# Clustered attention with an MLP: another order of the opening, with norms behind one-hot evictions and the first pair's scores between row maxima

## The chip, the cores and the metric

The kernel runs on one core of one Trainium2 chip. A core has a matmul engine (TensorE, PE in the profile; its weight loads are listed as PEld), VectorE (DVE), ScalarE (ACT), GpSimd (POOL) and SyncE (SP), which issues most of the DMAs; ACT issues a few. All of them work out of SBUF, PE writes to PSUM, and each engine takes its own instructions in program order. The metric is the device time of one execution in microseconds (us), lower is better; a kernel's time is the median over several executions.

## The reference

Attention in which a query sees only the keys of its own cluster, then a low-rank mix over the sequence, then a channel MLP with a residual. Batch 4, 8 heads, 768 positions, head size 64, 16 clusters, model size 512, hidden size 2048, all fp32:

```python
q_assign = np.argmax(np.einsum('bhsd,hcd->bhsc', q_n, c_n), axis=-1)   # q_n, k_n, c_n: rows of length 1
k_assign = np.argmax(np.einsum('bhsd,hcd->bhsc', k_n, c_n), axis=-1)
mask = q_assign[:, :, :, None] == k_assign[:, :, None, :]
scores = np.where(mask, scale * np.matmul(q, k.transpose(0, 1, 3, 2)), -1e9)
attn = softmax(scores)                     # row maximum taken off, exp, divided by the sum
x = np.matmul(attn, v)                     # then heads side by side: (B, S, 512)
u = x + (x^T @ U @ V)^T
out = u + np.maximum(u @ w_ch1, 0.0) @ w_ch2
```

## The kernel before

Two heads of one batch form a pair; there are 16 pairs, numbered from 0. Of every pair the program makes the same chain of steps, each a small function of the source:

- `load` brings queries and keys (tile `R`), `split_hi` (L375, ACT) and `split_lo` (L380, POOL or DVE) cut them into a high and a low part in a large tile `arena`, and `place_keys_hi`, `place_keys_lo`, `place_queries` (DMAs, L217) put the parts on the partitions where the matmuls want them.
- `sims` (L330 on PE, L333 on ACT) gives the similarity to the centroids; ACT's eviction multiplies by the centroids' inverse norms `c_rn`, which `norms` (L279 to L287, eight small DVE operations with one square root on ACT, L281) makes, once for pair 0's centroids and once for those of the three other pairs of heads. `turn_centroids` (L268, L271) transposes the centroids.
- `largest` and `clusters` (PE transposes L340, then five DVE operations L344, L345, L352, L353, L356) find the cluster of every query and key and write it as a one-hot tile `oh`.
- The one-hots go to partitions 64 to 96 of `arena`. For pair 0 alone this is `turn_clusters` (PE L422, evictions on ACT L429 and DVE L426). For the others it is `clusters_T` (six PE transposes L365, ACT eviction L367 to `ohT`) and `place_clusters` (four DMAs of `ohT` on SP's queue).
- `rowmax` (PE L440, DVE L442) makes, for 12 blocks of queries times two halves of the keys, the block of masked scores and its row maximum. `rowmax_T` and `rowmax_place` (L447, PE L452, ACT L454, a DMA of `mT` on ACT's queue) turn 6 or 12 columns of maxima into a row of `arena`, which the second matmuls of `scores` then subtract.
- `scores` (PE L464 and L466, exp on ACT L469 into `pr`), `weights` (sums of `pr` into `T`, L479, POOL and at a few places DVE) and `values` (PE L487, eviction L491) run 12 times per pair: two halves `h` of the queries, six key blocks `c` each. `sums`, `sums_T` and `normalise` finish the pair.

After the last pair of a batch come the mix, and after all pairs the MLP, which fills the second half of the time.

Nothing plans the order at run time. Each step is put in a list with a time (a plain number), the list is sorted by it, and the functions are called in that order; `keep_order` then ties each engine to the order of the calls. The times come from tables (one row per step, one column for pair 0, 1, 2, the last of a batch, the last of all and the rest). The first steps of all, on pairs 0 and 1, are written out by hand in the list `start`. Pair 0's scores have times from -0.47 up in steps of 1, its values come in groups of six, the transposes of pair 1's one-hots (`clusters_T`) have -0.09.

PSUM has four banks under the names `ps_...` and `o_ps`, and two tiles of two banks under `st`; a matmul into a bank waits until the bank's last reader is done.

Of the kernel before, what the change touches and what calls it, by code (L numbers as in the profile page):

```python
# [53 lines left out]
GV = 6  # L54
# [63 lines left out]
def clustered_attention_moe(ctx: ExitStack, tc: tile.TileContext, qk, v, cen, moe_U, moe_V, w1, w2, out):  # L118
# [820 lines left out]
    def at(time, fn, *args):  # L939
        plan.append((time, len(plan), fn, args))  # L940
# [3 lines left out]
        (table, AF.Sqrt), (load_centroids, 0, 1), (turn_centroids, 0), (load, 0, 0), (load, 0, 1),  # L944
        (load_centroids, 1, 4), (load, 1, 0), (load, 1, 1), (norms, 0, 1), (split_hi, 0, 0),
        (split_hi, 0, 1), (place_keys_hi, 0), (sims, 0), (split_lo, 0, 0), (split_lo, 0, 1),
        (constants, 0), (place_ones, 0), (largest, 0), (place_keys_lo, 0), (clusters, 0), (norms, 1, 4),
        (turn_centroids, 1), (turn_clusters, 0, 1), (place_queries, 0), (turn_centroids, 2),
        (turn_centroids, 3), (turn_clusters, 0, 0), (constants, 1), (sims, 1), (rowmax, 0, 0),
        (table, AF.Exp), (rowmax, 0, 2), (split_hi, 1, 0), (split_hi, 1, 1), (rowmax, 0, 5),  # L950
        (rowmax, 0, 1), (rowmax, 0, 4), (load_v, 0), (rowmax, 0, 3), (rowmax_T, 0, 0, 6),
        (rowmax_place, 0, 0, 6), (largest, 1), (split_lo, 1, 0), (split_lo, 1, 1), (clusters, 1),
# [7 lines left out]
    def kind(i):  # L960
        name = ("first", "second", "third")[i] if i < 3 else (
            "last" if i == n - 1 else "last of a batch" if i % NP == NP - 1 else "most")
        return kinds.index(name)

    def when(name, i):
        return NS * i + times[name][kind(i)]

    for i in range(n):
        if i > 1:
            for h in range(2):  # L970
                for fn in (load, split_hi, split_lo):
                    at(when(f"{fn.__name__}{h}", i), fn, i, h)
            for fn in (sims, largest, clusters, place_keys_hi, place_keys_lo, place_queries, place_ones):
                at(when(fn.__name__, i), fn, i)
        if i:
            for fn in (clusters_T, place_clusters, load_v):
                at(when(fn.__name__, i), fn, i)

        pace = (0.5, 0.75, 0.75, 1)[min(i, 3)]
        for u in range(NT if i == 0 else 0, NS):  # L980
            for h in range(2):
                if i < 3:
                    at(when("rowmax", i) + pace * u + 0.01 * h, rowmax, i, u, h)
                else:
                    g, r = divmod(2 * u + h, 2 * GV)
                    at(when("rowmax", i) + GV * g + spots[r], rowmax, i, u, h)
        if i == 1:
            at(when("rowmax_T", i) - 4, rowmax_T, i, 0, NT)
            at(when("rowmax_place", i) - 5, rowmax_place, i, 0, NT)
        u0 = NT if i < 2 else 0  # L990
        at(when("rowmax_T", i), rowmax_T, i, u0, NS)
        at(when("rowmax_place", i), rowmax_place, i, u0, NS)
        for k in range(NS):
            h, c = divmod(k, NT)
            at(when("scores", i) + k, scores, i, h, c)
            at(when("values", i) + GV * (k // GV) + GV - 1 + 0.001 * (k % GV), values, i, h, c)
            if c:
                at(when("weights", i) + k, weights, i, h, c)
        at(when("sums", i), sums, i)
        at(when("sums_T", i), sums_T, i)  # L1000
        for h in range(2):
            at(when(f"normalise{h}", i), normalise, i, h)
# [31 lines left out]
    for n_, (g, k) in enumerate((g, k) for g in range(NG) for k in range(2)):  # L1034
        c = M0 + (3 + 3.1 * n_ if n_ < 7 else 26.3)
# [17 lines left out]
    for b in range(1, B):  # L1053
# [17 lines left out]
        for k, (which, x) in enumerate(seq):  # L1071
# [20 lines left out]
            elif x < 6 or b < B - 1:  # L1092
                first = sorted(order[1].index(key) for key in order[b < B - 1][0:3])
# [44 lines left out]
```

## Time and profile before

| | |
|---|---|
| median of 3 runs | 1011.31 us (1010.62 to 1015.38) |
| profiled execution | 1008.9 us, of which 1007.1 us are the span of the profile |
| busy in the span: PE, DVE, ACT, POOL | 95%, 71%, 47%, 60% |
| attention (pairs 0 to 15) | from 0 to about 440 us |
| the opening that the change touches | from about 8 to 46 us |

The prediction shows lines of four views: the page; busy time by stretches (`us, PE busy (x) PEld busy (x) DVE busy (x) ACT busy (x) POOL busy (x), PEclk, DMA share, GB/s`, where PEclk is the granted clock of PE, 1 being full); the timeline (start in us, duration in us, engine, line, operation, tiles, sizes, count, and in brackets how long the engine sat idle before and what released it); and the order of the instructions. A row of the timeline with `x12` covers twelve instructions in a row and its duration is that of all twelve. A `q` behind an engine's name marks the queue that issues DMAs; the duration is that of the issuing.

### The profile page before, as it was taken

The page shows a single profiled execution, that of the slowest core. Times are in us where ns is not written, and L with a number is a line of the kernel's source. Part 1 is how long each engine was busy: PE and PEld are TensorE (multiplying, and loading weights), DVE is VectorE, ACT ScalarE, POOL GpSimd, SP SyncE. Part 2 cuts the span into 40 slices and gives each one's busy share as a digit, 9 for nine tenths or more (in the row PEclk, how much of TensorE's full clock was granted, in tenths as well). Part 3 has the DMA queues.
Part 4 walks back from the last instruction along what each step waited for, and adds up shares of the span by engine and source line. Part 5 has one row for each costly group of instructions (what it writes and reads, how often), then busy time and mean ns, then how long its engine had stood idle before and what let it go on. Part 6 is the DMA issues. An engine that isn't in the chain of part 4 may idle for free. (4 is left out here: it accounts for less than half of the span.)

```text
span 1007.1 us, 15377 instructions
## 1 busy us (share of the span) xinstructions
PE 953.1 (95%) x5368; PEld 778.0 (77%) x5368; DVE 715.1 (71%) x1322; ACT 472.0 (47%) x837; POOL 601.5 (60%) x453
## 2 busy tenths in 40 slices
PE   5899999999999999988988998999999899999997
PEld 3565665676666756656777887899999899999997
DVE  5797777777787667666788524765688666886767
ACT  4454555565555645464456534453344433443330
POOL 5466676889678868753356846742375623855330
PEclk9899999999999999989999999999999999999999
DMA  7754653655676644347477995877677776677744
GB/s 183 193 130 119 162 148 93 201 156 151 152 213 170 153 116 144 96 134 235 142 232 232 322 349 187 329 266 271 231 261 260 274 295 239 229 280 267 248 147 146
DMA packets 76733, 205.29 MB, mean 204 GB/s; under 512 B 8624, under 2 KB 42416, under 8 KB 71792
## 3 DMA queue, kind: packets, MB, share of 16 engines
q1 hardware_dynamic: 73968, 195.82, 60.9%
q10 hardware_dynamic: 2688, 8.49, 2.8%
q8 instruction: 42, 0.69, 0.3%
q14 instruction: 35, 0.29, 0.1%
HBM read 131.07 MB, written 41.94 MB: 172 GB/s over the span
## 5 line engine op out<-in xcount | busy, mean ns | idle before, releaser
L442 DVE TENSOR_REDUCE m<-ps_max 128x1 f32<-128x384 f32 x384 | 195.5, 549 | 82.6 <-PE ps_max L440 81.2
L479 POOL TENSOR_TENSOR T<-T,pr 128x768 f32<-128x768 f32 x120 | 225.7, 1881 | 46.1 <-ACT pr L469 19.5
L469 ACT ACTIVATE pr<-st 128x768 f32<-128x768 f32 x192 | 154.6, 813 | 85.7 <-PE st L466 69.0
L487 PE MATMUL o_ps<-pr,vt 128*64 128x384 f32 x768 | 132.9, 496 | 0.1
L440 PE MATMUL ps_max<-arena 128*128 128x384 f32 x384 | 126.6, 380 | 6.7 <-DVE oh L356 2.5
L464 PE MATMUL st<-arena 128*128 128x384 f32 x384 | 105.0, 354 | 1.9 <-ACT pr L469 1.8
L440 PEld LDWEIGHTS ps_max<-arena 128*128 128x128 f32 x384 | 70.5, 192 | 45.4 <-issue 21.4
L487 PEld LDWEIGHTS o_ps<-pr,vt 128*64 128x64 f32 x768 | 52.9, 138 | 66.9 <-issue 60.3
L466 PE MATMUL st<-arena 97*128 97x384 f32 x384 | 99.7, 341 | 4.6 <-DMA arena<-mT 2.6
L479 POOL TENSOR_TENSOR T<-pr 128x768 f32<-128x768 f32 x30 | 56.6, 1885 | 64.9 <-ACT pr L469 64.9
L464 PEld LDWEIGHTS st<-arena 128*128 128x128 f32 x384 | 66.3, 190 | 17.8 <-issue 9.9
L466 PEld LDWEIGHTS st<-arena 97*128 97x128 f32 x384 | 70.4, 190 | 6.2 <-issue 4.5
L491 ACT COPY os<-o_ps 128x384 f32<-128x384 f32 x32 | 15.4, 480 | 105.4 <-PE o_ps L487 105.4
L800 PE MATMUL ps_p<-arena,w 128*128 128x384 f32 x186 | 62.3, 335 | 0.1
L801 PE MATMUL ps_p<-arena,w 128*128 128x384 f32 x186 | 62.2, 334 | 0.0
L802 PE MATMUL ps_p<-arena,w 128*128 128x384 f32 x186 | 62.2, 334 | 0.0
L800 PE MATMUL ps_q<-arena,w 128*128 128x384 f32 x150 | 50.1, 334 | 0.0
L802 PE MATMUL ps_q<-arena,w 128*128 128x384 f32 x150 | 50.1, 334 | 0.0
L801 PE MATMUL ps_q<-arena,w 128*128 128x384 f32 x150 | 50.1, 334 | 0.0
L380 POOL TENSOR_TENSOR arena<-R,arena 128x768 fp32r<-128x768 f32 x18 | 34.4, 1918 | 13.5 <-ACT arena L375 7.9
L665 POOL TENSOR_TENSOR f<-f 128x512 f32<-128x512 f32 x8 | 10.3, 1293 | 52.1 <-DVE f L660 52.1
L607 DVE SCALAR_TENSOR_TENSOR hx<-ps_h,hx 128x384 fp32r<-128x384 f32 x32 | 17.7, 554 | 29.0 <-ACT hx L606 28.9
(541 smaller groups left out, 2444.3 us busy)
## 6 DMA issues: line engine op xcount, KB each, us to landing
w<-wc SPq DMA_DIRECT2D x24, 1024.0 KB
w<-wc SPq DMA_DIRECT2D x24, 768.0 KB
wc<-f SPq DMA_DIRECT2D x52, 256.0 KB
arena<-wc SPq DMA_DIRECT2D x17, 768.0 KB
R<-in_qk SPq DMA_DIRECT2D x32, 384.0 KB
arena<-arena SPq DMA_DIRECT2D x32, 384.0 KB
arena<-arena SPq DMA_DIRECT2D x64, 192.0 KB
arena<-wc SPq DMA_DIRECT2D x10, 1024.0 KB
```

The source lines that it names most:

```text
L380: eng.tensor_sub(part(X2[i % 3], 0, h), live["R", i][:, 2 * h:2 * h + 2].rearrange("p j q -> p (j q)"), part(X1[i % 3], 0, h))
L440: nc.tensor.matmul(ps[:, 0:HS], x1[:, 0, g // 2, g % 2, t * P:(t + 1) * P], x1[:, 1, h, g % 2, :], start=True, stop=True)
L442: nc.vector.reduce_max(live["m2", i][:, h, u:u + 1], ps[:, 0:HS], axis=AX.X)
L464: nc.tensor.matmul(st[:, j, 0:HS], x1[:, 1, hk, j, ks], x1[:, 0, h, j, :], start=True, stop=False)
L466: nc.tensor.matmul(st[:, j, 0:HS], x2[0:97, 1, hk, j, ks], x2[0:97, 0, h, j, :], start=False, stop=True)
L469: nc.scalar.activation(pr, st[:, :, 0:HS], AF.Exp, scale=SCALE)
L479: eng.tensor_add(T, live["p", i, h, 0] if c == 1 else T, live["p", i, h, c])
L487: nc.tensor.matmul(o_ps[64 * j:64 * j + 64, 0:HS], vv[:, c, j, :], pr[:, j, :], start=(c == 0), stop=(c == NT - 1))
L607: nc.vector.scalar_tensor_tensor(out=hl, in0=ps[:, 0:HS], scalar=0.0, in1=hh, op0=ALU.max, op1=ALU.subtract)
L800: nc.tensor.matmul(ps, w[:, 0, k], u[:, 0, k], start=(k == 0), stop=False)
L801: nc.tensor.matmul(ps, w[:, 0, k], u[:, 1, k], start=False, stop=False)
L802: nc.tensor.matmul(ps, w[:, 1, k], u[:, 0, k], start=False, stop=(k == 1))
```

## The change

Two edits, both in the order alone; every instruction is the same as before.

In the list `start`, the norms of the later centroids (`norms, 1, 4`) and their transposes move behind pair 0's one-hots (`turn_clusters`), and `sims` of pair 1 behind the first row maximum:

```diff
-        (constants, 0), (place_ones, 0), (largest, 0), (place_keys_lo, 0), (clusters, 0), (norms, 1, 4),
-        (turn_centroids, 1), (turn_clusters, 0, 1), (place_queries, 0), (turn_centroids, 2),
-        (turn_centroids, 3), (turn_clusters, 0, 0), (constants, 1), (sims, 1), (rowmax, 0, 0),
+        (constants, 0), (place_ones, 0), (largest, 0), (place_keys_lo, 0), (clusters, 0),
+        (turn_clusters, 0, 1), (place_queries, 0), (turn_clusters, 0, 0), (constants, 1), (turn_centroids, 1),
+        (rowmax, 0, 0), (turn_centroids, 2), (turn_centroids, 3), (norms, 1, 4), (sims, 1),
         (table, AF.Exp), (rowmax, 0, 2), (split_hi, 1, 0), (split_hi, 1, 1), (rowmax, 0, 5),
```

Pair 0's first six scores, exps and sums get times between those of the row maxima of its second half, and all its first values the time -2, which is ahead of `clusters_T` of pair 1:

```diff
         for k in range(NS):
             h, c = divmod(k, NT)
-            at(when("scores", i) + k, scores, i, h, c)
-            at(when("values", i) + GV * (k // GV) + GV - 1 + 0.001 * (k % GV), values, i, h, c)
+            first = i == 0 and h == 0
+            at(-8.99 + 0.5 * k if first else when("scores", i) + k, scores, i, h, c)
+            at(-2 if first else when("values", i) + GV * (k // GV) + GV - 1 + 0.001 * (k % GV), values, i, h, c)
             if c:
-                at(when("weights", i) + k, weights, i, h, c)
+                at(-8.7 + 0.5 * k if first else when("weights", i) + k, weights, i, h, c)
```

What this does to the engines, read from the built programs. On DVE, in the opening (`m_276` and `m_252` are the same tile of row maxima, `oh_127` is pair 0's one-hots), a minus stands before what is gone from a place and a plus before what is new there:

```order
 L356 TENSOR_TENSOR oh_127<-ps_simT,rank 128x24x16
+L426 TENSOR_SCALAR arena<-st,osc,obi 32x2x384 x2
+L442 TENSOR_REDUCE m_252<-ps_max 128x1 x2
 L279 TENSOR_TENSOR rw_g<-rw_g 128x192
 L280 TENSOR_REDUCE c_n_135<-rw_g 128x3
...
 L287 RECIPROCAL c_rn<-c_n_134 128x3
-L426 TENSOR_SCALAR arena<-st,osc,obi 32x2x384 x2
-L442 TENSOR_REDUCE m_276<-ps_max 128x1 x12
-L447 TENSOR_REDUCE m<-m_276 128x6
+L442 TENSOR_REDUCE m_252<-ps_max 128x1 x10
+L447 TENSOR_REDUCE m<-m_252 128x6
```

The eight operations of the norms, which stood ahead of the two evictions L426, now stand behind these and behind the first two of the twelve row maxima. The rest of DVE's order is as it was.

On PE, from the transposes for pair 1's clusters on, before (`oh_128` is pair 1's one-hots):

```order
L340 MATMUL ps_simT<-ident,sims 128x128 x3
L440 MATMUL ps_max<-arena 128x384 x12
L464 MATMUL st<-arena 128x384 x2
L466 MATMUL st<-arena 128x384 x2
L365 LDWEIGHTS oh_128
L365 MATMUL ps_oh<-ident_b,oh_128 128x128
```

and with the change, from the last of six scores on:

```order
L464 MATMUL st<-arena 128x384 x2
L466 MATMUL st<-arena 128x384 x2
L487 MATMUL o_ps<-pr,vt 64x384 x12
L365 LDWEIGHTS oh_128
L365 MATMUL ps_oh<-ident_b,oh_128 128x128
...
L452 MATMUL ps_mT<-ident,m 6x128
L330 MATMUL ps_sim<-R,cT 32x384 x4
L340 MATMUL ps_simT<-ident,sims 128x128 x3
L440 MATMUL ps_max<-arena 128x384 x6
L464 MATMUL st<-arena 128x384 x2
```

Before, pair 1's transposes L365 came behind one score of pair 0, and the five others, the values and a seventh score stood behind them, among L452, L330 and L340 of pair 2 and the row maxima L440 of pair 1. Now all six scores (spread among the last eight row maxima of pair 0) and the values stand ahead of L365; behind it there is no score until six row maxima of pair 1 are through. From the next row on PE's two orders are the same.

On ACT with the change, from the first exp on:

```order
L469 ACTIVATE pr<-st 128x768 x6
L491 COPY os<-o_ps 128x384
L367 ACTIVATE ohT<-ps_oh,obi,osc 128x768
L454 ACTIVATE mT<-ps_mT 6x128
L217 DMA arena<-mT 1x6x128
L333 ACTIVATE sims<-ps_sim,c_rn 128x384
L375 CAST arena<-R 128x768 x3
```

Before, the eviction L367 of pair 1's one-hots came behind the first exp, and L333 of pair 2 and the three casts L375 of later pairs stood between the others. SP issues the same DMAs in the same order as before.

## The prediction, made before the changed kernel was run

> **What bounds the kernel now.** I read the page first, then busy time by stretches, then the timeline of the opening engine by engine, since only the opening is edited.
>
> ```profile
> PE 953.1 (95%) x5368; PEld 778.0 (77%) x5368; DVE 715.1 (71%) x1322; ACT 472.0 (47%) x837; POOL 601.5 (60%) x453
> L469 ACT ACTIVATE pr<-st 128x768 f32<-128x768 f32 x192 | 154.6, 813 | 85.7 <-PE st L466 69.0
> ```
>
> ```profile
> 17.00:33.00 16.00, 11.61 (x32) 7.06 (x31) 14.68 (x31) 3.59 (x6) 3.59 (x2) 0.71 0.78 208
> 33.00:46.00 13.00, 12.23 (x73) 7.87 (x72) 7.63 (x14) 8.95 (x13) 9.73 (x5) 0.97 0.55 127
> 46.00:60.00 14.00, 13.60 (x80) 8.53 (x77) 11.58 (x21) 6.59 (x11) 7.02 (x5) 1.00 0.49 131
> 60.00:75.00 15.00, 14.06 (x75) 10.03 (x75) 14.15 (x34) 8.61 (x14) 11.01 (x7) 1.00 0.62 160
> 100.00:150.00 50.00, 49.19 (x299) 33.78 (x300) 37.76 (x76) 27.74 (x41) 34.99 (x20) 1.00 0.59 151
> ```
>
> PE is the bound of the whole. In the opening it is not: from 17 to 33 us DVE is (14.68 of 16), and from 33 to 46 us neither DVE nor ACT is full. From 46 us on PE or DVE is always nearly full. So a delay that exists at 46 us has hardly any hole to disappear in, and the question is when the first row that is common to both orders again can run: PE's L440 behind pair 0's first values, at 46.28. DVE's timeline up to there:
>
> ```profile
> 11.80 0.35 DVE L279 TENSOR_TENSOR rw_g<-rw_g 128x192 f32<-128x192 f32 x1
> 13.92 0.17 DVE L287 RECIPROCAL c_rn<-c_n 128x3 f32<-128x3 f32 x1
> 14.52 1.07 DVE L426 TENSOR_SCALAR arena<-st,osc,obi 32x768 fp32r<-32x768 bf16 x1 [0.42 <-ACT arena L429]
> 16.52 1.07 DVE L426 TENSOR_SCALAR arena<-st,osc,obi 32x768 fp32r<-32x768 bf16 x1 [0.93 <-ACT arena L429]
> 17.62 5.67 DVE L442 TENSOR_REDUCE m<-ps_max 128x1 f32<-128x384 f32 x12
> 23.33 0.17 DVE L447 TENSOR_REDUCE m<-m 128x6 f32<-128x12 f32 x1
> 27.01 0.56 DVE L356 TENSOR_TENSOR oh<-ps_simT,rank 128x384 bf16<-128x384 f32 x1
> 38.58 0.56 DVE L344 TENSOR_REDUCE mx<-ps_simT 128x24 f32<-128x384 f32 x1 [5.24 <-PE ps_simT L340]
> 39.65 2.87 DVE L442 TENSOR_REDUCE m<-ps_max 128x1 f32<-128x384 f32 x6
> 42.43 2.02 DVE L380 TENSOR_TENSOR arena<-R,arena 128x768 fp32r<-128x768 f32 x1
> 45.57 0.56 DVE L356 TENSOR_TENSOR oh<-ps_simT,rank 128x384 bf16<-128x384 f32 x1
> ```
>
> The norms (11.80 to 14.09) lie in a hole: the eviction behind them waits for ACT anyway, 0.42 us. The large hole is the 5.24 us before L344 of pair 2. PE:
>
> ```profile
> 18.24 3.70 PE L440 MATMUL ps_max<-arena 128*128 128x384 f32 x8 [0.36 <-DVE m L442]
> 27.71 4.31 PE L440 MATMUL ps_max<-arena 128*128 128x384 f32 x9 [2.25 <-DVE oh L356]
> 31.82 0.84 PE L464 MATMUL st<-arena 128*128 128x384 f32 x2
> 33.11 0.86 PE L365 MATMUL ps_oh<-ident_b,oh 128*128 128x128 bf16 x6
> 35.51 0.85 PE L330 MATMUL ps_sim<-R,cT 128*32 128x384 f32 x8
> 39.43 0.52 PE L464 MATMUL st<-arena 128*128 128x384 f32 x2
> 39.79 0.51 PE L466 MATMUL st<-arena 97*128 97x384 f32 x2
> 40.14 1.49 PE L440 MATMUL ps_max<-arena 128*128 128x384 f32 x4
> 42.26 4.09 PE L487 MATMUL o_ps<-pr,vt 128*64 128x384 f32 x24
> 46.28 0.30 PEld L440 LDWEIGHTS ps_max<-arena 128*128 128x128 f32 x2 [0.60 <-DVE oh L356]
> ```
>
> PE sits behind L356 twice: at 27.71 (pair 1's one-hots) and at 46.28 (pair 2's, done at 45.57 + 0.56 = 46.13). The chain that leads to the second starts with L365 at 33.11, and its other links are on ACT and in a queue:
>
> ```profile
> 16.80 0.58 ACT L333 ACTIVATE sims<-ps_sim,c_rn 128x384 f32<-128x384 f32 x1 [0.31 <-PE ps_sim L330]
> 18.80 1.55 ACT L375 CAST arena<-R 128x768 fp32r<-128x768 f32 x2
> 34.07 0.99 ACT L367 ACTIVATE ohT<-ps_oh,obi,osc 128x768 fp32r<-128x768 bf16 x1
> 35.09 2.62 SPq L217 DMA_DIRECT2D arena<-ohT  x4
> 35.65 0.25 ACT L454 ACTIVATE mT<-ps_mT 6x128 fp32r<-6x128 f32 x1
> 35.93 0.68 ACTq L217 DMA_DIRECT2D arena<-mT  x1
> 37.37 0.57 ACT L333 ACTIVATE sims<-ps_sim,c_rn 128x384 f32<-128x384 f32 x1
> 38.90 0.36 PEld L440 LDWEIGHTS ps_max<-arena 128*128 128x128 f32 x2
> ```
>
> Today PE does its scores while that chain runs.
>
> **Step 1, the norms.** Eight operations, 2.29 us from 11.80 to 14.09, free today, now between row maxima two and three, where DVE is the bound: +2.3. In return the second L429 no longer waits behind casts of L271, so L426 can end about half a microsecond sooner; the first L440 waits for copies by DMA too, which do not move. I give back 0.5 (between 0 and 0.6): **+1.8** (1.7 to 2.3). The first half of the maxima ends at 23.50 + 1.8 and L356 of pair 1 at 27.57 + 1.8 = 29.4; only PE transposes and five DVE operations lie between. Late behind the norms is also ACT's L333 of pair 1 (it needs `c_rn`: about 20.4 for 16.80), and with it the casts L375, POOL's L380 and SP's copies, by some 3.6 us. Their next reader on PE is pair 1's first row maximum, which comes later still (step 3). I cost that at nothing; without that cover it would be 3.6.
>
> **Step 2, PE from the gate to the end of the values.** The gate at 27.71 goes to 29.5. From there PE now does one L440, six scores, eight L440 in twos and 24 L487. At full clock two L464 take 0.36 (39.43 to 39.79), so do two L466 and two L440; a score is 0.71 (39.43 to 40.14); the values take 46.13 - 42.26 = 3.87. Sum: 0.18 + 6 x 0.71 + 4 x 0.36 + 3.87 = 9.75. DVE (0.47 per maximum, 5.67 / 12) keeps up, and so does ACT (813 ns an exp, in the second row of the page above). The values would end at 39.3. But the clock:
>
> ```profile
> 20.00:22.00 2.00, 1.84 (x5) 0.74 (x4) 2.00 (x6) 0.35 (x1) 2.00 (x2) 1.00 0.23 52
> 24.00:26.00 2.00, 1.47 (x6) 0.96 (x4) 1.39 (x3) 0.17 (x1) 0.00 (x0) 0.50 1.01 212
> 33.00:34.00 1.00, 1.00 (x8) 0.90 (x8) 0.31 (x2) 0.66 (x1) 0.00 (x0) 0.56 0.57 216
> 34.00:35.00 1.00, 1.00 (x7) 0.91 (x7) 0.00 (x0) 1.00 (x3) 0.00 (x0) 1.00 0.03 12
> ```
>
> PE runs at half clock from before 24 to about 33.9 us: it drops while the matmuls are paced by DVE, and is full again some 2 us after dense work began (31.82). A score at half clock takes 31.82 to 33.11, 1.29. The paced stretch stays, with gaps like today's, so I take half clock again, from 29.5 to about 33.9: 4.4 us of half work, 2.2 lost (bounds: 0, and 3.1 if it lasts the 6.2 us that went from 27.71 to 33.9). **Values end at 41.5** (39.3 to 42.4).
>
> **Step 3, the chain behind the values.** Call their end V. L365 and L367 took 33.11 to 35.06 = 1.95; with `os`'s eviction between but full clock I take 1.8 (1.6 to 2.3). Then two legs. Leg one: `ohT`'s DMAs until pair 1's first L440. Issued at 35.09, and at 38.90 L440 starts without a wait, so at most 3.8; the second issue alone is out 1.3 later, so at least 1.3; I take 3.0, plus 0.4 to the first maximum: V + 5.2. Leg two: L454 (0.25), the issue of `mT` (0.68), L333 (0.57), then what today runs from L333's end (37.94) to the first L442 (39.65), 1.71: with small gaps V + 5.1. So L442 starts at V + 5.2 (5.1 to 6.0). From its start to L356's end it is six maxima, L380 and three operations, 39.65 to 46.13 = 6.48, all on DVE: L356 ends at V + 11.7, and L440 runs at V + 11.85.
>
> **Sum.** 41.5 + 11.85 = 53.35 against 46.28: **+7.1 us**. Five scores and the values, 7.4 us of work, do go earlier on PE; the gain is lost since L365 goes from 33.11 to 41.5 and a chain of 11.9 us that had scores beside it now has almost nothing. From 46.28 on the orders are equal, and the stretches above show no hole; I carry 7.1 to the end. The profiled execution took 1008.9 (span 1007.1), so 1016.0 of its kind; the median of the runs is 2.4 above it, so the forecast is 1011.3 + 7.1 = **1018.4 us**.
>
> **A rule beside the rows.** The Trainium skill, "TensorE: Matmul & The Clock Gate", section "HAM oscillation — how this bites in real kernels", says that gaps of PE beyond about 3.4 us cost the clock. By that wording the gaps left here (none over 3 us ahead of the scores) would keep it full, which is the first rival; the rows show a drop with L440 still coming every 0.46 us until 21.94 (18.24 + 3.70) and PE at work again as soon as L447 is done at 23.50, so this trace speaks against the wording.
>
> **The rivals.**
>
> *The clock stays full.* Between 20.4 and 25 us DVE now paces row maxima where today PE falls idle at 21.94, so the use of PE in the stretch that decides may be just enough. Then V = 39.3, and the next L440 at 51.15: +4.9, 1016.2. Against it: the gap before the gate at 29.5 is as long as the 2.25 of today.
>
> *A second dip.* Between V + 1.6 and V + 11.85 PE has L330, L340, six L440 and one score, some 3.5 us of work in 10. If the clock falls there, the work from 53 us on, where PE is 13.60 of 14 busy, runs at half for 3 to 4 us: 1.5 to 2 more, +9, 1020.3.
>
> *Not slower: the chain is hidden.* One place decides, pair 1's first L440 after the values. If what it waits for came early enough that it went straight behind L340, PE would need from V = 39.3 on only L365, L452, L330 and L340 (about 2.2, by the 0.85 of L330 and the 0.86 of L365), six L440 at 0.47 and a score, and would reach the common row at 39.3 + 2.2 + 2.8 + 0.7 = 45.0: -1.3, 1010.0, no change. It needs L442 to start below V + 2.4, and pair 2's L356 to be no gate. For it speaks the work moved into the hole; against it that L367 cannot start before L365 is through PE, and that the copies alone are 1.3 at least.
>
> *The delay is swallowed later.* A hole bound by something the opening does not move (weights, transfers) could take it up. 100 to 150 us is 49.19 of 50 busy; I see none before the end of attention. It would be +1, 1012.5.
>
> That the order does not change as said is excluded by the rows of the built program.
>
> **How the numbers follow.** Forecast 0.46, full clock 0.18, second dip 0.15, swallowed 0.12, hidden 0.09. A measurement here cannot tell less than about 0.5%, 5 us, from no change. Slower by more: the forecast nearly whole, half of the full clock (its 1016.2 lies at the border, 1016.4), the dip: 0.67. Faster by more: a part of the hidden case, 0.05. The rest, 0.28, is no change. Range: from 1012.5 (the hidden case and some of the swallowed one left out) to 1021.5 (dip and slowest DMA); the forecast's own is 1016 to 1020.
>
> **What would show it.** DVE: the norms between L442 two and three, L356 of pair 1 ending near 29.4, a hole before L344 of pair 2 of about 8 us instead of 5.24. PE: L464 in twos between L440 from 29.5, at half clock until about 34; L487 ending near 41.5; L440 of pair 1 near 46.5 behind DMA `ohT`; an idle stretch ended by DVE L356 near 53. I am wrong if pair 1's L440 follows L340 at once, if the clock does not drop before the scores, or if the lag at the common row is gone by 100 us.

## The result, and the profile after

| | before | after |
|---|---|---|
| median of 8 runs each | 1011.57 us (1009.81 to 1015.38) | 1020.29 us (1015.32 to 1026.64) |
| ratio after to before | | 1.0081, 95% interval 1.0057 to 1.0105 |
| profiled execution, its span | 1008.9, 1007.1 | 1024.4, 1022.6 |

The change is slower by 8.2 us, 5.8 to 10.6 by the interval. The forecast was +7.1. The sum held; the trace of one execution shows that it is made of other items than the ones forecast.

The opening on PE, after (timeline; columns as in the prediction):

```profile
29.76 0.84 PE L464 MATMUL st<-arena 128*128 128x384 f32 x2
35.04 0.52 PE L464 MATMUL st<-arena 128*128 128x384 f32 x2
37.72 4.09 PE L487 MATMUL o_ps<-pr,vt 128*64 128x384 f32 x24
41.74 0.51 PE L365 MATMUL ps_oh<-ident_b,oh 128*128 128x128 bf16 x6
46.44 0.77 PE L440 MATMUL ps_max<-arena 128*128 128x384 f32 x3 [1.01 <-DMA arena<-ohT]
50.19 0.84 PE L440 MATMUL ps_max<-arena 128*128 128x384 f32 x2
50.83 0.82 PE L464 MATMUL st<-arena 128*128 128x384 f32 x2
52.44 0.41 PE L440 MATMUL ps_max<-arena 128*128 128x384 f32 x1 [0.25 <-DVE oh L356]
52.81 0.84 PE L330 MATMUL ps_sim<-R,cT 128*32 128x384 f32 x4
55.94 1.49 PE L330 MATMUL ps_sim<-R,cT 128*32 128x384 f32 x4 [2.28 <-DMA R<-in_qk]
65.81 4.09 PE L487 MATMUL o_ps<-pr,vt 128*64 128x384 f32 x24 [0.20 <-ACT ohT L367]
```

On DVE, after:

```profile
11.51 0.56 DVE L356 TENSOR_TENSOR oh<-ps_simT,rank 128x384 bf16<-128x384 f32 x1
18.01 0.35 DVE L279 TENSOR_TENSOR rw_g<-rw_g 128x192 f32<-128x192 f32 x1
28.60 0.56 DVE L356 TENSOR_TENSOR oh<-ps_simT,rank 128x384 bf16<-128x384 f32 x1
45.46 0.56 DVE L344 TENSOR_REDUCE mx<-ps_simT 128x24 f32<-128x384 f32 x1 [8.12 <-PE ps_simT L340]
46.89 2.88 DVE L442 TENSOR_REDUCE m<-ps_max 128x1 f32<-128x384 f32 x6 [0.19 <-PE ps_max L440]
49.68 0.95 DVE L380 TENSOR_TENSOR arena<-R,arena 128x768 fp32r<-128x768 f32 x1
51.74 0.56 DVE L356 TENSOR_TENSOR oh<-ps_simT,rank 128x384 bf16<-128x384 f32 x1
```

SP's queue, first of before, then of after:

```profile
42.07 1.22 SPq L320 DMA_DIRECT2D R<-in_qk  x1
```

```profile
43.36 2.61 SPq L217 DMA_DIRECT2D arena<-ohT  x4
46.02 0.82 SPq L217 DMA_DIRECT2D arena<-ones  x1
46.88 0.50 SPq L151 DMA_DIRECT2D rw<-in_U  x1
47.48 1.19 SPq L217 DMA_DIRECT2D arena<-arena  x2
48.71 1.63 SPq L320 DMA_DIRECT2D R<-in_qk  x1
```

And two common PE rows of before, behind the place where the prediction stopped:

```profile
47.87 0.85 PE L330 MATMUL ps_sim<-R,cT 128*32 128x384 f32 x8
55.81 4.09 PE L487 MATMUL o_ps<-pr,vt 128*64 128x384 f32 x24
```

To compare places in two traces I take the end of pair 0's one-hots as the common point (the first L356 of the DVE fence: 12.07 after, 11.88 before), so 0.19 is taken off each difference. What is left of a difference is called the lag of that place; it is read from one execution of each kernel. The lag of the change grows in four steps:

| place | before | after | lag |
|---|---|---|---|
| pair 1's one-hots done (L356) | 27.57 | 29.16 | 1.4 |
| pair 3's L330 starts | 47.87 | 52.81 | 4.8 |
| its second half | 48.22 | 55.94 | 7.5 |
| pair 0's second values (L487) | 55.81 | 65.81 | 9.8 |
| pair 1's first values | 76.09 | 86.09 | 9.8 |

(Before, the eight L330 stand as two fours, from 47.87 and from 48.22; the later four are taken for the second half. With the earlier four, 0.3 us would move from the fourth step to the third.)

The third row is a wait that the prediction does not have. L330 of pair 3 needs the second half of tile `R`. Its load is issued behind `ohT`'s copies on SP's queue, and these wait for the values: SP is busy without a hole from 43.36 until the load at 48.71, where before it was issued at 42.07: 6.4 later by the common point, for a use that comes 4.8 later. The semaphore that the load updates, read in the packed traces, gives its landing: before at 47.77, only 0.1 ahead of L330; after at 55.89, and L330 starts 0.05 behind it. PE stands for 2.28 us. The last step follows on that wait, by busy time in stretches, after:

```profile
52.00:54.00 2.00, 1.40 (x7) 0.33 (x5) 2.00 (x5) 0.81 (x1) 0.00 (x0) 1.00 0.84 230
54.00:56.00 2.00, 0.06 (x2) 0.06 (x4) 0.15 (x1) 0.00 (x0) 0.00 (x0) 0.73 1.06 237
56.00:58.00 2.00, 2.00 (x6) 0.76 (x7) 0.00 (x0) 0.46 (x1) 0.00 (x0) 0.50 0.55 120
58.00:60.00 2.00, 2.00 (x8) 2.00 (x7) 0.63 (x2) 0.93 (x2) 0.00 (x0) 0.50 0.74 203
60.00:62.00 2.00, 2.00 (x9) 1.91 (x8) 1.97 (x5) 0.39 (x1) 0.00 (x0) 0.56 0.00 0
```

In the wait the clock falls to half (such a stretch at half clock is called a dip), and then PE is full, at half clock, until nearly 62: what took 3.4 us before, from the second half of L330 at 48.22 to the next L452 at 51.59, takes 6.0 (55.94 to 61.89).

### The profile page after: what moved, and what is told of

Same layout as the page of the kernel before. It is cut to its first block, busy times and chain, and to the rows that moved or that the text cites. A ratio compares the mean times of both kernels' runs of the same rounds, so it can differ in the third digit from the quotient of the medians.

```text
span 1022.6 us, 15382 instructions
## 1 busy us (share of the span) xinstructions
PE 961.6 (94%) x5368; PEld 787.5 (77%) x5368; DVE 714.1 (70%) x1322; ACT 472.6 (46%) x837; POOL 600.7 (59%) x453
## 5 line engine op out<-in xcount | busy, mean ns | idle before, releaser
L479 POOL TENSOR_TENSOR T<-T,pr 128x768 f32<-128x768 f32 x120 | 225.9, 1882 | 56.3 <-ACT pr L469 33.9
L442 DVE TENSOR_REDUCE m<-ps_max 128x1 f32<-128x384 f32 x384 | 195.7, 548 | 89.0 <-PE ps_max L440 87.4
L440 PE MATMUL ps_max<-arena 128*128 128x384 f32 x384 | 127.4, 384 | 8.9 <-DVE oh L356 2.5
L487 PE MATMUL o_ps<-pr,vt 128*64 128x384 f32 x768 | 133.5, 498 | 0.2 <-ACT ohT L367 0.2
L464 PE MATMUL st<-arena 128*128 128x384 f32 x384 | 106.7, 360 | 2.2 <-ACT pr L469 2.1
L440 PEld LDWEIGHTS ps_max<-arena 128*128 128x128 f32 x384 | 72.5, 198 | 44.5 <-issue 21.4
L487 PEld LDWEIGHTS o_ps<-pr,vt 128*64 128x64 f32 x768 | 53.1, 139 | 67.4 <-issue 61.0
L464 PEld LDWEIGHTS st<-arena 128*128 128x128 f32 x384 | 68.0, 194 | 18.3 <-issue 10.6
L801 PE MATMUL ps_q<-arena,w 128*128 128x384 f32 x150 | 50.1, 334 | 0.0
L802 PE MATMUL ps_q<-arena,w 128*128 128x384 f32 x150 | 50.1, 334 | 0.0
L380 POOL TENSOR_TENSOR arena<-R,arena 128x768 fp32r<-128x768 f32 x18 | 33.8, 1881 | 19.8 <-ACT arena L375 10.9
```

Of the source, the lines that this page charges most:

```text
L440: nc.tensor.matmul(ps[:, 0:HS], x1[:, 0, g // 2, g % 2, t * P:(t + 1) * P], x1[:, 1, h, g % 2, :], start=True, stop=True)
L442: nc.vector.reduce_max(live["m2", i][:, h, u:u + 1], ps[:, 0:HS], axis=AX.X)
L464: nc.tensor.matmul(st[:, j, 0:HS], x1[:, 1, hk, j, ks], x1[:, 0, h, j, :], start=True, stop=False)
L479: eng.tensor_add(T, live["p", i, h, 0] if c == 1 else T, live["p", i, h, c])
L487: nc.tensor.matmul(o_ps[64 * j:64 * j + 64, 0:HS], vv[:, c, j, :], pr[:, j, :], start=(c == 0), stop=(c == NT - 1))
L801: nc.tensor.matmul(ps, w[:, 0, k], u[:, 1, k], start=False, stop=False)
```

## The experiments

Each kernel was timed against the kernel before on the same chip. In the tables "lag" is that of a place against the kernel before, from the common point; "time" is the ratio less 1, times the median of before (1013 us), with its 95% interval. Expectations that name a raw time mean the trace's own.

**One edit at a time.** First the list `start` alone, with scores and values at their old times:

```diff
-            at(-8.99 + 0.5 * k if first else when("scores", i) + k, scores, i, h, c)
-            at(-2 if first else when("values", i) + ..., values, i, h, c)
+            at(when("scores", i) + k, scores, i, h, c)
+            at(when("values", i) + ..., values, i, h, c)
...
-                at(-8.7 + 0.5 * k if first else when("weights", i) + k, weights, i, h, c)
+                at(when("weights", i) + k, weights, i, h, c)
```

> Only the list of first steps is changed (norms and centroid transposes behind pair 0's one-hots); pair 0's scores and values stay where they were before. Marks in the timeline: pair 1's one-hots end (second L356) at 27.57 us before and 29.16 with the change; pair 2's one-hots end (third L356) at 46.13 and 52.30. Theory (norms between row maxima lengthen DVE's chain, and nothing after them is late for another reason): second L356 ends near 29.2, everything behind it moves by the same 1.6, third L356 near 47.7, median +1.5 to +2.5 us. Rival (the norms are hidden, all of the loss is the place of the values): third L356 at 46.1 to 46.5, median within 0.5 us of before. Rival (the late casts and copies of pair 1 are what costs, 3.6 us): PE's L330 of pair 2 waits for R, third L356 at 49 or later, median +4.

Then the other edit alone, with `start` as before:

```diff
-        (constants, 0), (place_ones, 0), (largest, 0), (place_keys_lo, 0), (clusters, 0),
-        (turn_clusters, 0, 1), ..., (norms, 1, 4), (sims, 1),
+        (constants, 0), (place_ones, 0), (largest, 0), (place_keys_lo, 0), (clusters, 0), (norms, 1, 4),
+        (turn_centroids, 1), ..., (sims, 1), (rowmax, 0, 0),
```

> Only the second edit: pair 0's first scores between row maxima and its first values ahead of pair 1's transposes L365; norms as before. Theory (the chain from L365 to pair 2's one-hots starts only behind the values): second L356 ends at 27.6 as before, L487 ends near 40, third L356 near 50.5, and PE's L330 of pair 3 again waits for the DMA of R; median +5 to +8 us. Rival (most of the loss is the norms and the copies that they make late): third L356 below 48, median at most +2.

| | pair 1's one-hots | L330 of pair 3 | its second half | pair 1's first values | time |
|---|---|---|---|---|---|
| `start` alone | 1.4 | 1.3 | 1.3 | 1.1 | +0.4 (-1.8 to 2.5), 1014.02 |
| scores and values alone | 0.05 | 3.0 | 6.4 | 7.8 | +7.5 (5.2 to 9.8), 1019.52 |
| the change | 1.4 | 4.8 | 7.5 | 9.8 | +8.2 (5.8 to 10.6), 1020.29 |

The row of PE that waits, with scores and values alone:

```profile
54.58 0.84 PE L330 MATMUL ps_sim<-R,cT 128*32 128x384 f32 x4 [2.42 <-DMA R<-in_qk]
```

The norms cost 1.4 at the gate (the row maximum behind pair 1's one-hots) and 1.1 in the end, and with them alone L330 does not wait for `R`. The second edit has the rest, with the same two items, the wait for `R` (3.4 here) and the dip behind it (1.4). 1.1 and 7.8 make 8.9 of the 9.8.

**The values back.** The change, with pair 0's first values at their old time and the scores left early:

```diff
-            at(-2 if first else when("values", i) + ..., values, i, h, c)
+            at(when("values", i) + ..., values, i, h, c)
```

> The change, but pair 0's first values back at their time of before, which is behind six row maxima of pair 1; the scores stay between row maxima. L365 then stands right behind the sixth score. Theory (the 3.9 us of values ahead of L365 are on the chain): L365 near 37.8 instead of 41.7, third L356 near 48.4 instead of 52.3, values in the time in which DVE works for pair 2; median some 4 us below the change, +3 to +6 against before. Rival (the values only take the place of an idle PE, the chain is bound elsewhere): third L356 at 51 or later, median as the change, +8 to +10.

The timeline of this kernel, two rows of PE and one of DVE:

```profile
36.88 0.51 PE L365 MATMUL ps_oh<-ident_b,oh 128*128 128x128 bf16 x6
45.86 4.60 PE L487 MATMUL o_ps<-pr,vt 128*64 128x384 f32 x24
50.88 2.06 DVE L442 TENSOR_REDUCE m<-ps_max 128x1 f32<-128x384 f32 x4 [3.04 <-PE ps_max L440]
```

The chain starts 4.4 us sooner than in the change by the common point, and the third L356 ends at 47.84. But now the values stand behind the row maxima, and DVE waits 3.04 for the L440 queued behind the values. The load of `R` is in time, so the two other items are gone. L330 and everything after it lag 4.3; time +4.9 (2.8 to 6.9), 1017.16 us.

**The legs behind the values.** The change, with L365 ahead of the first score:

```diff
-                at(when(fn.__name__, i), fn, i)
+                at(-9.1 if i == 1 and fn is clusters_T else when(fn.__name__, i), fn, i)
```

> The change, but pair 1's transposes L365 (and with them ACT's L367) ahead of the first score instead of behind the values; values as in the change. This takes leg one (one-hots of pair 1 by ACT and DMA to pair 1's L440) off the path and leaves leg two (similarities of pair 2: L330, L333, L340, L344 behind the values). Theory (two legs of nearly the same length, 5.2 and 5.1 us): pair 1's L440 does not wait for DMA any more, but the third L356 is only about 1 to 1.5 us earlier than with the change, near 51; median -1 to -2 against the change. Rival (leg one alone is the cause): third L356 near 48.5 to 49, median 4 us or more below the change.

L440's wait for `ohT` is gone and the third L356 ends at 50.25, 1.7 sooner than in the change counted from the common point. The other leg now ends last: L344 waits 7.12 for L340 behind the values. The load of `R` is issued at 45.77, so the wait shrinks to 0.41, and no dip comes after it. Of the 5.7 that the lag is smaller than the change's (4.1 for 9.8), 1.7 come from the leg and 1.9 from the wait; the 2.1 that remain are about the size of the dip. Time +3.1 (1.1 to 5.2), 1016.09.

On top of that, pair 2's scores ahead of the values:

```diff
-                    at(when(f"{fn.__name__}{h}", i), fn, i, h)
+                    at(-7.5 + 0.1 * h if i == 2 and fn is load else when(f"{fn.__name__}{h}", i), fn, i, h)
...
-                at(when(fn.__name__, i), fn, i)
+                at(-2.3 if i == 2 and fn is sims else when(fn.__name__, i), fn, i)
```

> The change, with pair 1's transposes of the one-hots (L365) ahead of pair 0's first score as in the run before it, and now also pair 2's scores (L330, L333) ahead of the weighted values. Theory (two legs of nearly equal length hang behind the values; the earlier run took off one and its third L356 still ended at 50.25): with the other leg off too the maxima of pair 1 no longer wait for L344's chain, the third L356 ends near 48.0 (46.13 before, 52.3 in the change), the first values of pair 1 lag the kernel before by about +2 instead of +4.1, and the time is +1 to +3. Rival (DVE's row maxima or the clock set the place, not the legs): third L356 stays at 49.5 to 50.5, lag +4, time as in the earlier run, +3.

The timeline of this kernel, DVE and PE:

```profile
43.30 0.56 DVE L344 TENSOR_REDUCE mx<-ps_simT 128x24 f32<-128x384 f32 x1 [6.61 <-PE ps_simT L340]
53.46 1.49 PE L330 MATMUL ps_sim<-R,cT 128*32 128x384 f32 x4 [1.98 <-DMA R<-in_qk]
```

The theory of two legs missed: the third L356 ends at 50.12, as the rival had it, since L340 itself still stands behind the values on PE (it runs at 42.77, right behind them). L330 ahead of the values pushes them back by 1.6, and L344 gains only 0.4. The wait for `R` is back, with a dip from 52.8: its load stands on SP behind two copies of keys, these wait for ACT's casts L375, and the casts stand on ACT behind `os` of the values, which came later (load at 46.99, 1.2 later than with L365 first alone). Lag 7.8, which neither theory had; time +6.8 (4.1 to 9.4), 1021.01.

Last, everything early: the start list of before, L365 and pair 2's scores and transposes ahead, values at their old time:

```diff
-                at(-2.3 if i == 2 and fn is sims else when(fn.__name__, i), fn, i)
+                at({sims: -6.9, largest: -6.4}.get(fn, when(fn.__name__, i)) if i == 2 else when(fn.__name__, i), fn, i)
...
-            at(-2 if first else when("values", i) + ..., values, i, h, c)
+            at(when("values", i) + ..., values, i, h, c)
```

> The kernel before with its own start list (norms ahead), pair 0's first scores between the row maxima, the transposes of pair 1 (L365) ahead of them and pair 2's scores ahead of the gate, the weighted values at their old place. Theory (what the change lost is only the late chain and the norms' place, and the scores that go earlier are a gain once nothing hangs behind them): third L356 ends near 44 (46.13 before), first values of pair 1 1 to 2 us ahead of the kernel before, time -1 to -2, hardly to be told from no change. Rival (the clock is what decides: scores at half clock between maxima cost as much as they save): third L356 at 46 to 47, lag 0 to +1, time 0 to +2.

The timeline, DVE and PE:

```profile
42.76 2.60 DVE L380 TENSOR_TENSOR arena<-R,arena 128x768 fp32r<-128x768 f32 x1
46.48 0.56 DVE L356 TENSOR_TENSOR oh<-ps_simT,rank 128x384 bf16<-128x384 f32 x1
50.25 0.84 PE L330 MATMUL ps_sim<-R,cT 128*32 128x384 f32 x4 [1.23 <-DMA R<-in_qk]
```

The third L356 ends at 47.04, where the rival had it. L330 of pair 3 starts only 0.5 late, and then `R`, issued at 43.58, 1.7 later than before by the common point, costs 1.23 of waiting. Lag 2.4, time +1.2 (-1.1 to 3.5), 1013.99.

**The wait for `R`.** The change, with one DMA moved in SP's order, ahead of `ohT`'s copies:

```diff
-                    at(when(f"{fn.__name__}{h}", i), fn, i, h)
+                    at(1.62 if (i, h) == (3, 1) and fn is load else when(f"{fn.__name__}{h}", i), fn, i, h)
```

> The change, with one load moved: the second half of R of pair 3 is issued together with the other three loads of R, ahead of the copies of pair 1's and pair 2's keys on SP's queue. Theory (of the +10 at the second half's values, some 2.3 are a wait of L330 of pair 3 for that load, which had no slack before): the wait of 2.28 is gone, third L356 stays within 0.4 of 52.3, first values of pair 1 lag +7 to +7.5 instead of +9.8, time +6 to +7.5; and with no hole there perhaps no dip of the clock after 55. Rival (the hole only moves: the chain through DVE's row maxima behind it is late anyway, or the earlier load pushes back the copies of ohT): lag stays at +9 to +10, time +8 to +9.

PE's timeline, and busy time in the stretch behind it:

```profile
51.38 0.41 PE L440 MATMUL ps_max<-arena 128*128 128x384 f32 x1 [0.42 <-DVE oh L356]
51.75 0.85 PE L330 MATMUL ps_sim<-R,cT 128*32 128x384 f32 x8
```

```profile
51.40:59.50 8.10, 7.81 (x45) 5.51 (x45) 7.43 (x17) 5.14 (x8) 1.84 (x1) 1.00 0.55 135
```

The wait is gone, all eight L330 run together, and behind them the clock stays full. The lag is 3.8 instead of 9.8, well below the +7 to +7.5 expected: the wait (2.8) and the dip (2.3) both go. Another 0.7 is gone at L365 already, 0.4 of it at pair 1's one-hots, before the moved load is issued; in this execution the clock was full again at 33.0 instead of 34.4, so this part belongs to the execution and not to the edit. Time +3.7 (1.5 to 5.9), 1017.66.

**The dips.** Filler matmuls into PSUM that nobody reads keep PE busy where it would stand. First twelve in the wait itself, the load left where the change has it:

```diff
+    def filler(k, n=HS):
+        ps, x1 = ps_st.tile([P, 2, 512], F32, name="st"), X1[0]
+        for r in range(k):
+            nc.tensor.matmul(ps[:, r % 2, 0:n], x1[:, 1, 0, 0, 0:P], x1[:, 1, 1, 0, 0:n], start=True, stop=True)
+
+    def gaps(i):
+        yield from (0, 1)
+        if i == 3:
+            filler(12)
+        yield from (2, 3)
...
-        for s in range(4):
+        for s in gaps(i):
```

> The change with twelve matmuls that nobody reads in the hole between the two halves of L330 of pair 3, while PE waits for R's second half. Theory (of the +9.8 at pair 1's first values, 2.3 are the wait itself and about 2.3 the half clock from 55 to 62 which follows on it): the wait stays (L330's second half within 0.4 of 55.9), no dip behind it, lag +7.2 to +7.8. Rival (DVE's row maxima set the pace there, and the half clock costs nothing, as it did at 48 us): no dip, lag +9.5 to +10.

PE's timeline of this kernel, the filler (L484) and what follows, then busy time in the stretch after it:

```profile
53.23 2.36 PE L484 MATMUL st<-arena 128*128 128x384 f32 x12
55.52 0.84 PE L330 MATMUL ps_sim<-R,cT 128*32 128x384 f32 x4
```

```profile
55.00:62.00 7.00, 6.79 (x41) 5.15 (x39) 4.49 (x10) 3.87 (x6) 1.36 (x1) 1.00 0.30 82
```

The fillers ran over the wait: they end at 55.59 and L330 follows them without a wait, while the load, by its semaphore, had landed at 54.80. So here the fillers and not the load set L330's second half, by chance at the same lag as in the change, 7.5. No dip follows, and from there to pair 1's first values the lag grows by 0.1, to 7.6, where in the change it grew by 2.3. So the dip costs about 2.2, as the theory had it. Time +8.0 (5.5 to 10.5), 1021.84; the timed difference alone could not have shown this.

The other dip of the change, from 48.1 to 51.5, is another matter; the run with the load moved has it too, from 46.7 to 50.1. On top of the load moved first, nine fillers behind pair 2's L330 and two and two among the six row maxima:

```diff
+    for time, k in ((2.7, 9), (4.655, 2), (5.41, 2)):
+        at(time, filler, k)
```

> The run with the load moved, and beside it matmuls that nobody reads on PE (9 behind pair 2's L330, 2 and 2 among pair 1's row maxima): work is added so that PE is busier where it waits behind the values. Theory (the half clock from 48 us on, which follows on the waits there, costs 1 to 1.5 us): no dip at 48, first values of pair 1 1 to 1.5 us sooner than in the run without them, lag +5.5 to +6.5. Rival (the clock there costs nothing, since DVE sets the pace of that stretch): dip gone or not, lag the same or up to 0.5 more for the added matmuls.

Busy time in the stretch of that dip, first with the load moved alone, then with these fillers:

```profile
46.00:51.00 5.00, 4.65 (x15) 3.75 (x14) 4.93 (x10) 1.26 (x3) 1.16 (x1) 0.66 0.78 186
```

```profile
46.00:51.00 5.00, 4.34 (x21) 3.55 (x21) 4.76 (x9) 2.10 (x5) 1.83 (x1) 1.00 0.73 183
```

No dip, and no gain: lag 4.4 against 3.8 without fillers, and 0.6 of that stands already at L365 (8.3 against 7.7), ahead of the first filler; from there on the lag shrinks by 3.9 in both. DVE is full there either way, 4.93 and 4.76 of 5. The rival held: half clock where DVE set the pace cost nothing here. Time +3.8 (1.4 to 6.2), 1017.32.

**The half clock ahead of the values.** The change with fillers among pair 0's first row maxima and in the two waits ahead of the gate:

```diff
-        (rowmax, 0, 1), (rowmax, 0, 4), (load_v, 0), (rowmax, 0, 3), (rowmax_T, 0, 0, 6),
+        (rowmax, 0, 1), (filler, 2, 192), (rowmax, 0, 4), (filler, 2, 192), (load_v, 0), (rowmax, 0, 3), (filler, 6), (rowmax_T, 0, 0, 6),
...
+    at(-9.015, filler, 9)
```

(and `(filler, 2, 192)` behind the row maxima 2 and 5).

> The change with the same matmuls among pair 0's first row maxima and ahead of the gate, none among its scores. Theory (half clock from the gate at 29.3 to 34.4 costs 2.2 us, the term of the prediction): clock full at the gate, L365 behind the values at 39.3 to 39.8 instead of 41.7, third L356 2 us sooner (50.2), and what hangs behind it (the wait for R of pair 3, the dip after 55) by as much or less, so first values of pair 1 lag +7 to +8 instead of +9.8. Rival (the values' end is set by DVE's maxima and ACT's exponentials, not by PE's clock): L365 at 41 to 42 with the clock full.

PE's timeline:

```profile
29.79 0.51 PE L464 MATMUL st<-arena 128*128 128x384 f32 x2
39.67 0.51 PE L365 MATMUL ps_oh<-ident_b,oh 128*128 128x128 bf16 x6
54.01 0.84 PE L330 MATMUL ps_sim<-R,cT 128*32 128x384 f32 x4 [2.45 <-DMA R<-in_qk]
```

Two L464 take 0.51 at the gate instead of 0.84, and L365 comes at 39.67: 2.0 sooner, the 2.2 of the prediction's second step. At L330 of pair 3 the lag is 2.7. The wait for `R` is still there, since the whole queue moved with the values, but this time no dip follows, as busy time behind the wait shows:

```profile
54.00:61.00 7.00, 6.74 (x38) 5.11 (x38) 5.00 (x11) 4.39 (x7) 1.83 (x1) 1.00 0.31 84
```

Nothing filled this hole, and it is longer than the change's (2.45 for 2.28): that PE stands about this long does not by itself bring the dip. Lag 5.8, time +4.3 (1.5 to 6.9), 1017.06. The expected 7 to 8 had kept the dip.

The same fillers in the kernel before, with two more of 192 columns behind each of the last four pairs of its second row maxima:

> The kernel before with matmuls that nobody reads on PE in the opening (two of 192 columns behind each pair of L440, six of 384 while PE waits for L447, nine while it waits for L356), so that the clock does not drop at 23.6; 61% more work on PE there, none elsewhere. Theory (the half clock from 23.6 to 33.8 costs about 1 us, since DVE paces PE until 31.8): clock full throughout, L340 of pair 1 and the first score sooner, L365 at 32.2 to 32.6 instead of 33.1, pair 1's first values 0.8 to 1.5 us sooner, time -1, hardly to be told from no change. Rival (the fillers take PE as much as the clock gives back, or the clock drops all the same): lag 0 to +1.

PE's timeline, and busy time around the gate:

```profile
31.53 0.54 PE L464 MATMUL st<-arena 128*128 128x384 f32 x2
32.26 0.51 PE L365 MATMUL ps_oh<-ident_b,oh 128*128 128x128 bf16 x6
```

```profile
24.00:34.00 10.00, 8.80 (x50) 7.03 (x48) 8.55 (x18) 1.75 (x3) 0.00 (x0) 1.00 0.93 265
```

The clock stays full and every place from L365 on to pair 4's first values is 0.9 to 1.0 us sooner. Time -2.8 (-4.9 to -0.8), 1010.80 against 1013.17, ratio 0.9972 (0.9952 to 0.9992). The interval leaves out no change, by little, as one of thirteen intervals; of the size, the opening in the trace explains 1.0.

Last, all of it together: scores between the row maxima with everything else early (the run above), the load moved first, and the fillers, the nine of them ahead of L365:

```diff
+                    at(1.62 if (i, h) == (3, 1) and fn is load else -7.5 + 0.1 * h if i == 2 and fn is load else when(f"{fn.__name__}{h}", i), fn, i, h)
...
+    at(-9.105, filler, 9)
```

> The order with the scores between the row maxima, but with nothing left hanging behind the values (norms at their old place, L365 and pair 2's scores ahead, values at their old place), the second half of R of pair 3 loaded with the other halves, and the matmuls that nobody reads in the opening. Theory (the moved scores as such give nothing, since the row maxima on DVE and the values set the place of L330 of pair 3; what the filled kernel before gained came from the clock): no wait for R, L330 of pair 3 lags the kernel before by -1.2 to +0.2, first values of pair 1 as much, time -2.5 to 0, no better than the filled kernel before (-2.4). Rival (with every wait gone, the scores that go earlier pay too): lag -2 or less, time below -3.

No wait for `R`; L330 of pair 3 leads the kernel before by 1.4 and pair 1's first values by 1.7, 0.4 to 0.7 more than the filled kernel before. This lies between theory and rival. It is one execution of each, and loads and pair 2's similarities moved as well, so that the early scores pay is not shown. The timing does not tell it from no change: -0.5 (-2.6 to 1.5), 1012.74 against 1013.76.

**Does the opening's lag reach the end?** Over the thirteen kernels:

| kernel | lag at pair 1's first values | time |
|---|---|---|
| the change | 9.8 | 8.2 |
| `start` alone; scores and values alone | 1.1; 7.8 | 0.4; 7.5 |
| values back; L365 first | 4.3; 4.1 | 4.9; 3.1 |
| both legs; all early | 7.8; 2.4 | 6.8; 1.2 |
| load first; with fillers | 3.8; 4.4 | 3.7; 3.8 |
| filled wait; filled ahead of the gate | 7.6; 5.8 | 8.0; 4.3 |
| before, filled; all together | -1.0; -1.7 | -2.8; -0.5 |

No pair differs by more than 1.8 us, and the differences have both signs; the intervals of the times reach some 2 us to each side. The traces say the same without that spread: at pair 14's first values (L487 at 424.52 before, 434.24 with the change) the change is 9.5 behind, and in twelve of the thirteen the lag there is within 1.1 of the one in the table. In the other, load first with fillers, it grows by 1.9, with a dip at 310.7 on the way. So the opening's lag is carried through the attention.

## Why the prediction was right, and where it was not

*Step 1, the norms: right in place, a little too dear.* They stand between row maxima two and three (18.01), and pair 1's L356 ends at 29.16 for the 29.4 forecast. The term was 1.8; the run with `start` alone puts it at 1.4 at the gate and 1.1 at the end.

*Step 1, the late copies "at nothing": right.* With `start` alone nothing waits for them, and the lag goes from 1.4 to 1.1.

*Step 2, gate and clock: right.* The values were to end at 41.5; L365 starts at 41.74, right behind them. The clock was half from the gate on, and full at 34.4 for the 33.9 assumed. That it costs about 2.2 is shown by the filled change, 2.0. The rival "the clock stays full" has its V there, 39.3 forecast and 39.67 measured.

*Step 3, the legs: right up to L442, wrong behind it.* L442 starts at 46.89, V + 5.2 as forecast, and the hole before L344 is 8.12 where "about 8" was said. From L442 to L356's end 6.48 was forecast and 5.41 measured, all of it L380: 0.95 for 2.02. And the gate itself was misread. I took the 0.60 before the weight load at 46.28 for a wait of PE for L356. PE was then at the end of its 24 L487 (42.26 + 4.09), so the wait cost nothing. In the change the common L440 runs at 50.19, ahead of L356; of the four L440 in that place only the fourth waits for it, at 52.44. So a score and three L440 slip ahead of the gate, and L330 starts 0.51 behind L356's end instead of 1.74 before. Together, 1.1 and 1.2, these take the forecast +7.1 to the 4.8 that was there at L330.

*Step 3 and the sum, the load behind `ohT`: this step failed.* Step 3 followed the copies of `ohT`, late behind the values, to PE's L440 and no further, and the sum carried its 7.1 to the end because the stretches show no hole. The second half of pair 3's `R` is issued after `ohT` on SP's queue. Before, 6.15 us lay between its issue at 42.07 and its use at 48.22, and it landed at 47.77, so it had next to no slack. In the runs in which PE waits for it, it comes 6.2 to 8.1 us after its issue (45.77 to 52.02 with L365 first, 46.49 to 54.58 with scores and values alone). Issued 6.4 later for a use 4.8 later it was 2.3 late on PE, 2.8 in lag. The load moved ahead takes the wait away. The norms are not needed for it: with scores and values alone, the norms at their old place, PE waits 2.42.

*The sum.* 7.1 was forecast at the common row and carried to the end. True were 3.7 at that row (50.19 for 46.28) and 4.8 at L330, then 2.8 of wait for `R` and 2.3 of dip. The errors stood against each other: that the sum was right is luck, the account behind the values was not right. Whether the dip followed in the other executions of the change too is not seen.

*The rivals.* The second dip came where its rival had put it, from 48.1 to 51.5, and cost nothing. A third, behind the wait for `R`, cost 2.3, for the 1.5 to 2 that the rival had assumed. "Hidden" did not happen: pair 1's L440 waits for `ohT`, 1.01 us. "Swallowed later" did not happen: at pair 14's values 9.5 of the 9.8 are there.

*The rule beside the rows.* The Trainium skill, "TensorE: Matmul & The Clock Gate", section "HAM oscillation — how this bites in real kernels", speaks of idle gaps beyond about 3.4 us. Here the clock fell in a hole of 2.28 us, and did not fall where the same hole was filled; the trace does not agree, a shorter gap is enough here, as it was in the kernel before. Nor does the length of the gap alone decide: in the hole of 2.45 us in the change with fillers ahead of the gate the clock stayed full. What decides was not tried. The same page of the Trainium skill, section "What's actually happening", has the activity window run free of the program; the clock's rise at 34.4 in the change and at 33.0 in the same stretch with only a later load moved agrees with it.

## What to carry to other kernels

When a step moves later, follow the queue on which it issues its DMAs to the first load behind them, and ask how much slack that load has at its use; here a load for two pairs later, with the dip behind it, cost as much as the chain that had been counted. A releaser named in brackets is a gate only if the engine had nothing left to run: hold the wait against the end of the row before it, and look whether the rows behind are already through when the releaser moves. Half clock cost 2.2 us where PE set the pace and nothing where DVE did, so price each dip by who is full in that stretch.

## What the runs showed of the hardware that was not expected

*The column of the granted clock can say full when it is half.* Of the change, and of the change with fillers ahead of the gate, the same stretch:

```profile
28.00:34.00 6.00, 4.69 (x15) 4.72 (x16) 4.41 (x10) 1.61 (x2) 0.00 (x0) 1.00 0.96 245
```

```profile
28.00:34.00 6.00, 4.91 (x28) 4.62 (x27) 5.86 (x13) 2.57 (x4) 1.36 (x1) 1.00 0.96 233
```

Both say 1.00. But the pair of L464 takes 0.84 in the first and 0.51 in the second. In the profile of the change the clock has no entry before 34.4; until its first entry the column shows full, and the duration of a known matmul is the better witness.

*DVE's L380 takes 0.95 us or more than twice that, by what POOL does.* POOL beside it, in the kernel before and in the run with everything early (there DVE's L380 is the 2.60 above):

```profile
43.60 2.54 POOL L380 TENSOR_TENSOR arena<-R,arena 128x768 fp32r<-128x768 f32 x1
```

```profile
42.73 1.83 POOL L380 TENSOR_TENSOR arena<-R,arena 128x768 fp32r<-128x768 f32 x1
```

In the second, POOL starts first and takes its usual 1.83, to 44.56; DVE, there at 42.76, ends at 45.36, 0.8 after that. In the first, DVE is there at 42.43 while POOL's operation before runs to 43.60, ends at 44.45, and POOL's next takes 2.54 instead of 1.83. In the change POOL's L380 is over at 48.2 and DVE takes 0.95 at 49.68. The two take turns whole operation by whole operation. The Trainium skill, "SBUF — State Buffer", section "SBUF: two separate sides", says this: a DVE operation with two SBUF inputs and a POOL operation that reads SBUF exclude each other for the whole instruction. The trace agrees to about 0.2 us; so 1.1 of the 2.02 I had put into the sum was POOL, not work.

*Dips far from any edit.* In the mix and the MLP the change's profile has dips that the profile before has not (480 to 495 us: 0.77 against 1.00; 788 to 808: 0.91 against 1.00), and other kernels here have them at other places. The change's profiled execution was 15.5 us over that of before, its median 8.7. What starts such a dip was not tried. One profile's end holds them all, so a lag at a place common to two traces, ahead of them, is the better measure of an edit in the opening.
